# The first pixels of a spatial-reduction attention kernel, loaded by two queues in place of one

## The chip, the core and the metric

The kernel runs on one core of a Trainium2 chip. The core has a matrix engine (TensorE, PE in the profile), a vector engine (VectorE, DVE), an engine for activation functions (ScalarE, ACT), a general engine (GpSimd, POOL) and SyncE (SP), which mostly issues DMAs. DMAs are issued by an engine into its own queue (SP's, ACT's and POOL's appear below) and are moved by 16 DMA engines. The metric is the device time of one execution in microseconds (us): the median of several runs.

## What is computed

The reference has two stages. The first is attention with spatially reduced keys: `kv` (4 images of 384 x 32 pixels, 128 channels) is averaged over blocks of 4 x 4 pixels, which leaves 768 keys per image, and multiplied by `w_sr`; the result is keys and values at once.

```python
kv_pool = kv.reshape(B, H // r, r, W // r, r, C).mean(axis=(2, 4))
kv_flat = kv_pool.reshape(B, -1, C) @ w_sr
k = v = kv_flat
s = scale * (q @ k.transpose(0, 2, 1))
a = softmax(s)                      # with 1e-09 added to the sum
out = a @ v
```

The second stage is a feed-forward layer over all 4 x 12288 = 49152 rows: `h = x @ w_in` (128 to 2048), `g = h * sigmoid(1.702 h)`, `g @ w_out` (2048 to 128). Inputs and output are float32; the kernel computes in bf16 with float32 sums.

## The kernel before

The rows are worked in 96 groups of 512. A group's attention has six chunks of 128 keys: one matmul per chunk gives scores (L398), ACT takes their exponential (L400), and matmuls with the values, which carry a column of ones for the sum, follow (L412). The feed-forward stage has 16 chunks of 128 hidden units per group (L674, ACT's activation at L676, L684). Two rounds alternate: attention for half of the groups, then their feed-forward stage, then the same for the other half. ACT's work is a row of large activations, each of two or three banks of PSUM; PE fills the banks of one while ACT reads those of another. The order of all instructions is written out by the program itself: a planner with estimated costs places small jobs (pooling, transposing q, keys and values) between the large ones, and each engine executes its instructions strictly in the order in which they were written.

The change lies at the very beginning. The keys of image 0 are made from six chunks of pixels, each 128 rows of 2048 values (4 rows of 4 pixels make a key). Chunk 0 is loaded as float32 by SP's queue (L287) into `first_f`, a part of the big tile `x`, and cast to bf16 by DVE and ACT in five pieces (`cast_first`, L320 to L326): DVE casts columns 0 to 512, 512 to 1024 and 1792 to 2048, ACT casts 1024 to 1536 and 1536 to 1792. Behind it SP's queue loads `w_sr` (L289). All else is loaded by POOL's queue, which casts on the way: the first pieces of q (`load_q`, L264) and chunks 1 to 5 (`load_chunk`, L143), in this order: q group 0, q group 1, chunk 1, q groups 2 and 3, q groups 4 and 5, chunks 2 to 5.

While the loads are under way DVE makes an identity matrix and a matrix `sum4` that adds four rows (L304 to L318), and PE runs 13 matmuls on ones (`warm`, L335). Then the order on PE is:

- pool chunk 0 (16 matmuls at L152, four for each quarter of the columns, in the order of quarters 0, 2, 1, 3), transpose q group 0 (L278), one warm matmul, the keys of chunk 0 (L184), transpose q group 1;
- scores of group 0 with chunk 0 (L398), the values of chunk 0 (L189), one warm matmul, scores of group 1 with chunk 0 (L398);
- pool chunk 1 (L152), two warm matmuls, keys and values of chunk 1 (L197, L198), one warm matmul, transpose q group 2, scores of groups 0 and 1 with chunk 1 (L398), and so on.

On DVE the result of each of these is copied out of PSUM: `pTc` (L155), `kT` (L185, L199), `v` (L190, L200), `qT` (L284; for group 0 the copy is ACT's, L282). ACT's order at the beginning: load of its function table, the two casts of L325, the copy of L282, the exponentials of groups 0 and 1 with chunk 0 (512 columns each), then exponentials of 1024 columns.

Completion of a DMA is told by a semaphore; DMAs of SP's and ACT's queues take eight such semaphores in turn.

Of the kernel before, what the change touches and what calls it, by code (L numbers as in the profile page):

```python
# [24 lines left out]
def kernel(  # L25
    ctx, tc, q, kv, w_sr, moe_w_in, moe_w_out, out,
):
    nc = tc.nc
# [26 lines left out]
    kv_r = kv.rearrange("b (ch p) (a w) c -> b a ch p (w c)", p=128, a=2)  # L55
# [228 lines left out]
            nc.vector.tensor_copy(dst, src)  # L284

    first_f = x[:, 0:2 * SG].bitcast(F32)
    nc.sync.dma_start(out=first_f, in_=kv_r[0, 0, 0])  # L287
    w_sr_f = kvs[:, 0, 0, :]
    nc.sync.dma_start(out=w_sr_f, in_=w_sr)  # L289
    load_q(0, 0, 1)  # L290
# [23 lines left out]
    for m in range(0, 128, 32):  # L314
        p = slice(m, m + 32)
# [655 lines left out]
```

## Time and profile before

| what | value |
|---|---|
| time, median of 3 runs | 945.8 us (945.44 to 945.89) |
| span of the profiled execution | 943.6 us (the page gives no other time of it) |
| PE busy | 936.7 us, 99% of the span |
| ACT busy | 929.0 us, 98% |
| DVE busy | 688.6 us, 73% |
| POOL busy | 66.9 us, 7% |
| DMA, mean over the span | 106 GB/s |
| load of chunk 0, SP's queue | 1024 KB, 4.8 us from issue to landing |
| load of chunk 1, POOL's queue | landed 7.0 us after its issue at 2.52 us |
| ACT's first exponential | 8.38 us |
| ACT's third exponential | 12.00 us, after 2.32 us without work |

The profile is of one execution; times in it count from the start of the span. A row of the timeline has the start, the duration, the engine and the line, the operation with its output and input, how many instructions the row merges, and in brackets how long the engine had idled before and what ended that. A row of the chain has a start, a duration, and what the end of the kernel was waiting for in that time. Ends of matmuls are modelled: back to back ones overlap in their tails.

### The profile page before, as it was taken

Reading aid. Unit: us, or ns where it says so; the run is one execution under the profiler, and the core shown is the slowest. Engines: PE = TensorE matmul, PEld = TensorE weight load, DVE = VectorE, ACT = ScalarE, POOL = GpSimd, SP = SyncE. Lnnn points to the kernel's source line nnn. Section 1 sums busy time; section 2 is a strip of 40 time slices with the busy share of each in tenths; the row PEclk is TensorE's granted clock in tenths of the full one; section 3 lists DMA queues with packets and bytes.
Section 4 is the critical chain, followed back from the end, with each engine's and each line's share of the span. In section 5 each row is a group of like instructions: output and inputs, shape, how many; then the busy total and the mean of one; then the engine's idle time right before and its main releaser. Section 6 shows DMA issues by size and latency. Waiting matters only on the chain.

```text
span 943.6 us, 15502 instructions
## 1 busy us (share of the span) xinstructions
PE 936.7 (99%) x6218; PEld 499.8 (53%) x6218; DVE 688.6 (73%) x1261; ACT 929.0 (98%) x722; POOL 66.9 (7%) x117
## 2 busy tenths in 40 slices
PE   8999999999999999999999999999999999999998
PEld 4777776444444444445447777744444444444444
DVE  5677755767667788878787657588988779877851
ACT  6999999999999999999999999999999999999997
POOL 3101014200003320000000000000000000000000
PEclk9999999999999999999999999999999999999999
DMA  9998999947679993665235674462222121222222
GB/s 211 240 277 161 180 174 117 133 88 168 132 138 177 171 121 65 106 108 102 56 57 113 129 163 97 106 123 43 37 37 42 34 45 34 41 39 38 41 37 53
DMA packets 379464, 99.91 MB, mean 106 GB/s; under 512 B 353536, under 2 KB 376960, under 8 KB 378272
## 3 DMA queue, kind: packets, MB, share of 16 engines
q1 hardware_dynamic: 350784, 64.06, 36.2%
q0 software_dynamic: 28336, 34.74, 21.9%
q8 instruction: 48, 0.79, 0.3%
q14 instruction: 24, 0.20, 0.1%
q10 hardware_dynamic: 272, 0.13, 0.0%
HBM read 52.49 MB, written 49.81 MB: 108 GB/s over the span
## 4 chain that ended last, share of the span: by engine, by line
PE 92%; ACT 6%; DVE 1%; DMA 1%; issue 0%; POOL 0%; POOLq 0%
PE banks L684 35%; PE banks L674 35%; PE banks L412 11%; PE banks L398 9%; ACT ag L400 6%; DMA x<-in_kv_dram 1%; PE banks L469 1%; PE banks L463 1%; PE banks L712 0%; PE banks L152 0%; DVE x L443 0%; DVE ea L503 0%; PE banks L197 0%; POOL x L264 0%; PE banks L278 0%
## 5 line engine op out<-in xcount | busy, mean ns | idle before, releaser
L676 ACT ACTIVATE ag<-banks 128x1536 bf16<-128x1536 f32 (+1 forms) x506 | 676.3, 1510 | 0.0
L674 PE MATMUL banks<-x,w_both 128*128 128x512 bf16 x1509 | 408.2, 379 | 0.2 <-ACT ag L400 0.2
L684 PE MATMUL banks<-ag,w_both 128*128 128x512 bf16 x1493 | 405.5, 379 | 0.0
L400 ACT ACTIVATE ag<-banks 128x1536 bf16<-128x1536 f32 (+2 forms) x208 | 245.7, 1409 | 3.7 <-PE banks L398 3.2
L684 PEld LDWEIGHTS <-w_both 128*128 128x128 bf16 x1520 | 148.6, 98 | 179.0
L674 PEld LDWEIGHTS <-w_both 128*128 128x128 bf16 x1509 | 146.6, 98 | 172.0 <-issue 0.7
L412 PEld LDWEIGHTS <-ag 128*128 128x128 bf16 x2264 | 146.8, 98 | 47.9 <-issue 0.2
L412 PE MATMUL banks<-v,ag 128*128 128x129 bf16 x2264 | 166.0, 220 | 0.0
L398 PE MATMUL banks<-qT,kT 128*128 128x512 bf16 x542 | 150.8, 379 | 1.1 <-DVE kT L199 0.4
L695 DVE STREAM_TRANSPOSE o_sb<-banks 128x512 f32<-128x512 f32 x95 | 66.9, 705 | 70.4 <-PE banks L684 68.5
L503 DVE SCALAR_TENSOR_TENSOR ea<-ea,eb 128x512 f32<-128x512 f32 x136 | 93.0, 684 | 5.4 <-issue 2.1
L534 DVE RECIPROCAL eb<-ea 128x256 f32<-128x256 f32 x54 | 92.5, 1729 | 0.9
L527 DVE SCALAR_TENSOR_TENSOR ea<-ea,eb 128x512 f32<-128x512 f32 x108 | 73.8, 684 | 2.9
L440 DVE RECIPROCAL rec<-banks 128x3 f32<-128x3 f32 x122 | 21.8, 178 | 68.4 <-PE banks L412 67.8
L443 DVE TENSOR_TENSOR x<-banks,rec 128x384 bf16<-128x384 f32 x122 | 67.9, 557 | 4.2
L398 PEld LDWEIGHTS <-kT 128*128 128x128 bf16 x542 | 45.7, 97 | 20.8 <-issue 1.2
L514 DVE TENSOR_SCALAR qT<-banks 128x512 f32<-128x512 f32 x27 | 18.7, 692 | 39.5 <-PE banks L463 39.5
L492 DVE TENSOR_SCALAR ea<-banks 128x512 f32<-128x512 f32 x34 | 23.5, 691 | 29.1 <-PE banks L469 29.0
L209 POOL DMA_DIRECT2D kvs<-in_kv_dram x32 | 40.3, 1260 | 56.9 <-DMA kvs<-in_kv_dram 56.4
L697 POOL DMA_DIRECT2D out_dram<-o_sb x2 | 1.3, 674 | 519.1 <-DVE o_sb L695 519.1
L584 POOL MEMSET gate_tile<- 1x1 f32 x38 | 8.1, 214 | 285.4 <-DVE gate_tile L583 285.3
L498 DVE SCALAR_TENSOR_TENSOR eb<-eb,ea 128x512 f32<-128x512 f32 x34 | 23.5, 690 | 1.0
(95 smaller groups left out, 355.2 us busy)
## 6 DMA issues: line engine op xcount, KB each, us to landing
out_dram<-o_sb SPq DMA_DIRECT2D x378, 64.0 KB, 1.9
kvs<-in_kv_dram POOLq DMA_DIRECT2D x32, 384.0 KB, 6.6
q_bf<-in_q_dram POOLq DMA_DIRECT2D x21, 512.0 KB, 9.3
x_bf<-x SPq DMA_DIRECT2D x13, 768.0 KB, 5.5
x<-in_kv_dram POOLq DMA_DIRECT2D x6, 512.0 KB, 12.5
x<-in_kv_dram POOLq DMA_DIRECT2D x3, 1024.0 KB, 11.0
x_bf<-x SPq DMA_DIRECT2D x6, 384.0 KB, 4.0
x<-in_kv_dram SPq DMA_DIRECT2D x1, 1024.0 KB, 4.8
```

What stands on the lines that cost most here:

```text
L209: nc.gpsimd.dma_start(out=kv_sums[b][:, i2], in_=kv_p[b, i, w, :, i2], **({"accum_op": ADD} if n else {}))
L398: nc.tensor.matmul(ps[:, k, :], kTs[i // GB][:, jc * 128:(jc + 1) * 128], rhs, start=True, stop=True)
L400: nc.scalar.activation(place([("a",) + c for c in chunks]), ps, AF.Exp, scale=scale)
L412: nc.tensor.matmul(av_of[u][:, k * (C + 1):(k + 1) * (C + 1)], weights(("a", i, jc))[:, o:o + T], vs[i // GB][:, jc, 0:C + 1], start=(jc = ...
L443: nc.vector.tensor_tensor(to, ps[:, :, 0:C], rec.unsqueeze(2).broadcast_to([128, TS, C]), MUL)
L503: nc.vector.scalar_tensor_tensor(a, a, COEFFS[k], b, ADD, MUL)
L527: nc.vector.scalar_tensor_tensor(a, a, COEFFS[k], b, ADD, MUL)
L534: nc.vector.reciprocal(b[:, m:m + 256], a[:, m:m + 256])
L674: nc.tensor.matmul(ps[:, k, :], w_in_sb[:, fc * 128:(fc + 1) * 128], x[:, g % (4 * XS) * G:(g % (4 * XS) + 1) * G], start=True, stop=True)
L676: nc.scalar.activation(place([("m",) + c for c in chunks]), ps, AF.Gelu_apprx_sigmoid)
L684: nc.tensor.matmul(o_of[g], w_out_sb[:, fc, :], weights(("m", g, fc)), start=(fc == 0), stop=(fc == FCH - 1))
L695: nc.vector.transpose(o_sb, o_of.pop(g))
```

## The change

The 128 rows of the load of chunk 0 are issued as two DMAs of 64 rows: rows 0 to 63 by SP's queue as before, rows 64 to 127 by ACT's queue, which stands ahead of all other work of ACT. Nothing else is edited.

```diff
     first_f = x[:, 0:2 * SG].bitcast(F32)
-    nc.sync.dma_start(out=first_f, in_=kv_r[0, 0, 0])
+    for queue, p in ((nc.sync, slice(0, 64)), (nc.scalar, slice(64, 128))):
+        queue.dma_start(out=first_f[p], in_=kv_r[0, 0, 0][p])
     w_sr_f = kvs[:, 0, 0, :]
     nc.sync.dma_start(out=w_sr_f, in_=w_sr)
     load_q(0, 0, 1)
```

In the changed program every line behind the edit has a number that is higher by one.

## The prediction

> **What bounds the kernel now.** I read the engine table first, then the timeline of the first 16 us, the waits, and the chain that ended last.
>
> ```profile
> PE 936.7 (99%) x6218; PEld 499.8 (53%) x6218; DVE 688.6 (73%) x1261; ACT 929.0 (98%) x722; POOL 66.9 (7%) x117
> ```
>
> ScalarE (ACT) and TensorE (PE) are both full; ACT's idle time is 943.6 - 929.0 = 14.6 us. The timeline shows where most of that lies, around these lines:
>
> ```profile
> 0.75 1.28 ACT L325 ACT_TABLE_LOAD   x1 [0.75 <-PEq L955]
> 0.75 0.41 SPq L287 DMA_DIRECT2D x<-in_kv_dram  x1
> ...
> 5.61 0.93 ACT L325 CAST x<-x 128x512 bf16<-128x512 f32 x2 [3.58 <-DMA x<-in_kv_dram]
> 5.61 0.98 DVE L325 CAST x<-x 128x512 bf16<-128x512 f32 x3 [2.18 <-DMA x<-in_kv_dram]
> ...
> 6.90 0.29 DVE L155 CAST pTc<-banks 128x128 bf16<-128x128 f32 x1 [0.17 <-PE banks L152]
> ...
> 8.38 1.29 ACT L400 ACTIVATE ag<-banks 128x512 bf16<-128x512 f32 x2 [0.67 <-PE banks L398]
> ...
> 8.65 0.39 PE L398 MATMUL banks<-qT,kT 128*128 128x512 bf16 x1
> ...
> 9.56 0.56 PE L152 MATMUL banks<-sum,x 128*128 128x32 bf16 x16 [0.52 <-DMA x<-in_kv_dram]
> ...
> 12.00 4.73 ACT L400 ACTIVATE ag<-banks 128x1024 bf16<-128x1024 f32 x5 [2.32 <-PE banks L398]
> ```
>
> The bracket is the idle time before the row and what ended it. ACT idles 0.75 + 3.58 + 0.59 (before the L282 copy) + 0.67 + 2.32 = 7.9 us before 12.00, and about 5.95 us behind 937.4 (2.70 before its last copy, and from the end of that copy at 940.35 to the end of the span). From 12.00 to 937.4 only 14.6 - 7.9 - 5.95 = 0.7 us are left. So whatever moves the exponential at 12.00 moves the end of the kernel, nearly one to one; what moves anything earlier counts only as far as it moves that one. What sets 12.00, by the chain:
>
> ```profile
> 2.52 7.00 DMA x<-in_kv_dram
> 9.52 0.05 issue
> 9.56 0.56 PE banks L152 x16
> 10.13 0.54 PE banks L335 x2
> 10.66 0.16 PE banks L197
> ```
>
> This is the load of chunk 1 by POOL's queue, not the load that is changed (chunk 0). The two meet on PE: its instructions stand in order, so L152 for chunk 1 comes behind everything that chunk 0 needs, the last of which is the score matmul at 8.65. Two such matmuls in a row take 0.60 for 0.39 each, so one holds the array 0.21 us and PE could have begun L152 at 8.86. It began at 9.56. **Chunk 0 therefore has 0.70 us to spare.**
>
> **The change part by part.** The load itself: the same 1 MB, the same rows, on two queues. Packets of SP's queue, counted up to 3.5, 4.25 and 5.0 us, are 50, 93 and 130; two of the last are of w_sr. So the 128 rows of 8 KB are through at about 5.0, and the landing is recorded at 0.75 + 4.8 = 5.55, some 0.55 later. From 4.25 to 5.0 some 35 rows of 8 KB pass, near 390 GB/s. POOL's queue has its first packet at 5.2, though it was issued at 1.29: it begins when the rows are through. The pixels thus already use the DMA engines nearly alone.
>
> The issue on ACT: the one DMA that ACT issues in this trace took 0.417 us (L723). It now stands ahead of the table load, in time in which ACT waits anyway: cost 0. SP's issue of w_sr cannot come later than now, and w_sr_sb (6.51) isn't on the path: 0. Later DMAs of SP turn to the next of eight completion semaphores; one transpose gets another wait, for a DMA of tens of us before: 0.
>
> **The added wait** is what matters. The first casts on DVE and on ACT now need both halves, and in the built program each has one wait of its own, the other standing ahead of it as a separate instruction. On DVE nothing lies between. On ACT the order becomes: issue of ACT's half; wait for SP's half; table load; cast, which waits for ACT's half. Before, the table load ran from 0.75 to 2.03, inside the wait for pixels. Now it begins when SP's half lands. Its price is 1.28 us, by this row and by the two later ones (1283 ns each at L676). Behind it in ACT's queue are the two casts of L325 (0.93 together), the copy of qT at L282 and all exponentials; PE's L152 waits for the third and fourth quarter of the pixels from those casts.
>
> Let X be the landing of SP's half. ACT's cast begins at X + 0.06 (5.61 - 5.55) + 1.28, and S, its delay, is X + 1.34 - 5.61 = X - 4.27. The rest of chunk 0 hangs on it link by link (last cast 6.54, pTc 6.90, kT 7.61, score matmul 8.65), so L152 for chunk 1 begins at the later of 9.56 and 8.86 + S.
> - Lower end of X: SP's 64 rows all go first. The 64th packet falls at 3.5 + 0.75 x 14/43 = 3.74, so X = 4.3, S = 0: no cost.
> - Upper end: the rows alternate to the end, X = 5.55, S = 1.28, L152 at 10.14, 0.58 late.
> - I take X = 5.4: SP issued at 0.75 and ACT, whose table load began at 0.75, is free at the same moment, so alternation is nearest; SP's queue may lead a little. S = 1.13, L152 at 9.99, **+0.43 us**.
>
> ACT's own half binds only if it lands after 5.4 + 1.34 = 6.74, 1.2 us later than the whole load now. DVE's casts would end at 6.6 to 6.8, before ACT's at 7.67. The two early exponentials, 8.38 to 9.67, slide to about 9.5 to 10.8, still before 12.4.
>
> Sum: 943.6 + 0.4 = 944.0 of span. The page has no time beside its span; the median of the three runs shown, 945.8, is 2.2 above it, and I keep that: **946.2 us**, 0.05% slower. For this kernel 0.2% (1.9 us) is about what can be told from no change, so my forecast is: no difference.
>
> [...]
>
> **Rivals.**
> 1. *Hidden altogether.* SP's half lands by 4.97 (S up to 0.70), so the chunk 1 load still sets L152. For it: SP's rows may be read first. Against: equal starts. Time 945.8 (945.6 to 945.9).
> 2. *Faster.* The load begins slowly: 20 packets by 2.75, where the later rate of 43 in 0.75 us would have given 57 from 1.75 on. If that ramp is one queue's and two fill it, the rows end up to 37/57 = 0.65 us sooner, POOL's queue begins sooner and chunk 1 lands at 8.87. With X = 4.75, S = 0.48, PE is ready at 9.34: L152 0.22 earlier, 945.6; with SP's half well ahead too, 0.65, 945.15. Against: the ramp may be the memory's, and POOL's queue may find two queues ahead of it.
> 3. *The table load costs more than its row.* Working it as a cost of twice its row, S = 1.13 + 1.28 = 2.41, L152 at 11.27, +1.7, 947.5. Against: at 141.50 a table load follows an activation that ended at 141.48, and the next begins at 142.79; nothing but 1.28 us shows. [...]
> 4. *Slower by more than 0.2%, by PE's clock.* The 13 first matmuls (L335) start 0.43 apart until 3.90 and then about 0.21 apart: PE starts at half speed and takes 2.9 us of work to leave it. They end at 5.35; now PE does four small matmuls and waits some 1.1 us for ACT's first cast, where before its gap was 0.73. If that sends it back to half speed, 2.9 us of work at half speed loses 1.45, and about twice that if it comes in the dense stretch behind 12 and needs a second such stretch: 946.2 + 1.45 to 2.9 = 947.7 to 949.1. It decides from the gap at which the clock falls; gaps of 0.7 us at 5.35 and 8.9 left it up in this trace. [...]
>
> **How the numbers follow.** Forecast (+0.1 to +0.9) 0.62; hidden 0.16; faster rival 0.08; dearer table load 0.05; clock 0.09. The clock case and a little of the third lie above 947.7: slower by over 0.2%, 0.10. Even the faster rival stays within 0.2%; 0.02 for faster. The rest, 0.88, is within. The range goes from the middle of the faster rival, 945.3, past the forecast's upper end (946.4, and 0.3 for the scatter of 945.44 to 945.89) to half of the third, 947.1; it leaves out about 0.04 below and 0.13 above.
>
> **What would show it.** The table load on ACT at 5.3 to 5.6 instead of 0.75, and the cast behind it near 6.7. L152 of chunk 0 with a wait of about 1 us for ACT in its middle. L152 for chunk 1 near 10.0, waiting for PE's own order and not for a DMA; the exponential at 12.4. ACT full from there on. The prediction is wrong if the table load still stands before the wait, if SP's half lands below 5.0, if chunk 1 lands more than 0.4 us away from 9.52, or if the matmuls between 6 and 12 stand 0.43 apart.

## The result: slower by 0.37%, and the profile after

The changed kernel takes 948.46 us (five executions: 948.05, 948.19, 948.46, 950.75, 950.98) against 945.89 before (the median of five); the ratio is 1.0037, with a 95% interval of 1.0026 to 1.0047. The executions fall into two groups, near 948.2 with a mean granted PE clock of 0.998 and near 950.8 with 0.996. The profiled one took 950.75 and has a span of 949.0, 5.4 us above that of before. Its beginning, from the timeline (lines of the changed program are higher by one):

```profile
0.76 0.56 ACTq L288 DMA_DIRECT2D x<-in_kv_dram  x1
0.76 0.58 SPq L288 DMA_DIRECT2D x<-in_kv_dram  x1
...
8.67 1.28 ACT L326 ACT_TABLE_LOAD   x1 [8.67 <-DMA x<-in_kv_dram]
8.70 1.02 DVE L326 CAST x<-x 128x512 bf16<-128x512 f32 x3 [5.27 <-DMA x<-in_kv_dram]
...
9.97 0.93 ACT L326 CAST x<-x 128x512 bf16<-128x512 f32 x2
10.64 0.49 PEld L152 LDWEIGHTS <-x 128*128 128x128 bf16 x12 [1.29 <-ACT x L326]
...
13.99 0.61 PE L399 MATMUL banks<-qT,kT 128*128 128x512 bf16 x1
...
14.39 0.63 PE L152 MATMUL banks<-sum,x 128*128 128x32 bf16 x16
...
17.52 1.02 ACT L401 ACTIVATE ag<-banks 128x1024 bf16<-128x1024 f32 x1 [2.28 <-PE banks L278]
```

The table load has moved behind the wait, as forecast. But the wait ends at 8.6, where it ended at 5.55. ACT's third exponential stands at 17.52 in place of 12.00: 5.52 late, and the span is 5.4 longer. That this exponential carries the end nearly one to one was right.

The issues with their times to landing show which half is late:

```profile
x<-in_kv_dram ACTq DMA_DIRECT2D x1, 512.0 KB, 5.2
x<-in_kv_dram SPq DMA_DIRECT2D x1, 512.0 KB, 7.8
```

SP's 512 KB needed 7.8 us where the whole 1024 KB needed 4.8. Packets by queue (count, MB, share of the time of 16 DMA engines) say why; a packet is counted in the stretch in which it starts. Before, from 3.25 to 4.25 us:

```profile
q1 hardware_dynamic: 54, 0.44, 106.4%
```

After, from 3.25 to 4.25 us (q10 is ACT's queue):

```profile
q10 hardware_dynamic: 29, 0.23, 103.9%
```

After, from 5 to 6 us (q1 is SP's queue):

```profile
q1 hardware_dynamic: 27, 0.22, 101.2%
```

The time of one packet is the share times 16 engines times the stretch, over the count: 1.064 x 16 / 54 = 0.315 us before, 1.012 x 16 / 27 = 0.600 us after. The engines are as busy as before, and each 8 KB row takes nearly twice as long. Nor do the two queues run side by side: ACT's 64 rows have all started by 4.26 us, when SP's first starts, and SP's last starts near 6.7.

PE's clock, lastly (the columns are the stretch, busy times by engine, the granted clock, the DMA share and GB/s):

```profile
8.00:9.00 1.00, 0.00 (x0) 0.00 (x0) 0.30 (x1) 0.33 (x1) 0.00 (x0) 1.00 1.30 228
9.00:10.00 1.00, 0.27 (x4) 0.17 (x4) 0.85 (x4) 0.99 (x2) 0.90 (x2) 0.81 1.09 221
10.00:12.00 2.00, 1.36 (x17) 0.84 (x17) 0.32 (x2) 1.20 (x3) 0.39 (x2) 0.50 1.08 196
12.00:14.00 2.00, 2.00 (x10) 0.69 (x9) 1.27 (x4) 0.83 (x2) 1.19 (x2) 0.50 1.26 216
14.00:16.00 2.00, 2.00 (x21) 0.85 (x21) 0.29 (x1) 0.65 (x2) 0.51 (x1) 0.50 1.07 215
16.00:18.00 2.00, 1.82 (x13) 0.92 (x15) 1.40 (x4) 0.48 (x1) 0.57 (x2) 0.89 1.06 213
```

From about 9.6 to 16.5 PE runs at half speed; before, the column has 1.00 in all of the first 18 us. The column does not show the slow start, in which it has 1.00 as well. The warm matmuls do (before, then after):

```profile
0.96 4.39 PE L335 MATMUL banks<-ones 128*32 128x512 bf16 x13 [0.96 <-DVE col L307]
0.97 5.55 PE L336 MATMUL banks<-ones 128*32 128x512 bf16 x13 [0.97 <-DVE col L308]
```

Before, they begin 0.43 apart and from 3.90 about 0.21 apart; here all thirteen lie 0.43 apart, so PE had not left half speed when the last of them began.

### The profile page after: what moved, and what is told of

The parts are those of the page before. It is cut to its first block, busy times and chain, and to the rows that moved or that the text cites. A ratio compares the mean times of both kernels' runs of the same rounds, so it can differ in the third digit from the quotient of the medians.

```text
span 949.0 us, 15391 instructions
## 1 busy us (share of the span) xinstructions
PE 933.4 (98%) x6104; PEld 500.8 (53%) x6218; DVE 689.1 (73%) x1261; ACT 929.1 (98%) x722; POOL 66.8 (7%) x117
## 4 chain that ended last, share of the span: by engine, by line
PE 55%; ACT 42%; DVE 1%; DMA 1%; issue 1%; ACTq 0%
ACT ag L677 36%; PE banks L685 18%; PE banks L675 17%; PE banks L413 9%; PE banks L399 9%; ACT ag L401 6%; DMA x<-in_kv_dram 1%; PE banks L464 0%; PE banks L713 0%; PE banks L278 0%; PE banks L336 0%; DVE x L444 0%; PE banks L152 0%; PE banks L470 0%; DVE ea L504 0%
## 5 line engine op out<-in xcount | busy, mean ns | idle before, releaser
L675 PE MATMUL banks<-x,w_both 128*128 128x512 bf16 x1468 | 403.0, 379 | 1.7 <-ACT ag L401 0.2
L685 PE MATMUL banks<-ag,w_both 128*128 128x512 bf16 x1465 | 399.9, 379 | 1.8
L399 PE MATMUL banks<-qT,kT 128*128 128x512 bf16 x497 | 145.7, 379 | 2.5 <-DVE kT L199 0.4
```

Of the source, the lines that this page charges most:

```text
L399: nc.tensor.matmul(ps[:, k, :], kTs[i // GB][:, jc * 128:(jc + 1) * 128], rhs, start=True, stop=True)
L675: nc.tensor.matmul(ps[:, k, :], w_in_sb[:, fc * 128:(fc + 1) * 128], x[:, g % (4 * XS) * G:(g % (4 * XS) + 1) * G], start=True, stop=True)
L685: nc.tensor.matmul(o_of[g], w_out_sb[:, fc, :], weights(("m", g, fc)), start=(fc == 0), stop=(fc == FCH - 1))
```

## The experiments

Open were: whether two queues or two halves of 64 rows make the rows slow, and what of 64 rows; what the table load behind the wait costs; and what PE's clock costs. Diffs are against the changed kernel unless said otherwise.

**Halves on one queue, columns on two, alternate rows on two.** These three and the next ran on one chip, where the kernel before took 945.48.

Both halves on SP's queue:

```diff
-    for queue, p in ((nc.sync, slice(0, 64)), (nc.scalar, slice(64, 128))):
+    for queue, p in ((nc.sync, slice(0, 64)), (nc.sync, slice(64, 128))):
```

> Both halves of 64 rows are issued by SP's queue, one behind the other. Theory R (a DMA into 64 adjacent partitions moves each 8 KB row in about 0.6 us per DMA engine in place of 0.31 to 0.38, whichever queue it is on): the 128 rows are through at 6.2 to 6.8 us, the second half lands at 6.8 to 8.6, and the time is 947 to 951 us. Theory Q (two hardware queues at once are what is slow): the rows are through at 5.0 to 5.3, the second half lands at 5.5 to 5.8, and only the table load behind the wait is left, 945.8 to 946.5 us.

950.59 us, ratio 1.0054 (1.0040 to 1.0068). One queue is no faster than two. Its packets from 3.25 to 4.25 us:

```profile
q1 hardware_dynamic: 28, 0.21, 95.1%
```

0.951 x 16 / 28 = 0.54 us. The table load begins at 9.58, later than the forecast of this run.

All 128 rows on both queues, cut by columns:

```diff
-    for queue, p in ((nc.sync, slice(0, 64)), (nc.scalar, slice(64, 128))):
-        queue.dma_start(out=first_f[p], in_=kv_r[0, 0, 0][p])
+    for queue, c in ((nc.sync, slice(0, SG // 2)), (nc.scalar, slice(SG // 2, SG))):
+        queue.dma_start(out=first_f[:, c], in_=kv_r[0, 0, 0][:, c])
```

> The same two queues, but each loads 1024 of the 2048 columns of all 128 rows (pieces of 4 KB). ACT's casts need ACT's half alone, so the table load stands before the wait again. Theory R: both halves land by 5.8 us and the time is 945.3 to 946.2. Theory Q: the second half lands at 7 us or later and the time is 947 to 950.

945.56 us, ratio 1.0001 (0.9993 to 1.0010): no different from before. Its packets (4 KB) from 3.25 to 4.25 us and its issues:

```profile
q1 hardware_dynamic: 53, 0.22, 54.2%
q10 hardware_dynamic: 50, 0.20, 50.7%
```

```profile
x<-in_kv_dram ACTq DMA_DIRECT2D x1, 512.0 KB, 5.0
x<-in_kv_dram SPq DMA_DIRECT2D x1, 512.0 KB, 5.2
```

0.542 x 16 / 53 = 0.164 us for 4 KB, the speed of before, with both queues at work. Two queues do no harm here; loads of 64 neighbouring rows do.

Even rows on SP, odd rows on ACT:

```diff
-    for queue, p in ((nc.sync, slice(0, 64)), (nc.scalar, slice(64, 128))):
+    for queue, p in ((nc.sync, slice(0, 128, 2)), (nc.scalar, slice(1, 128, 2))):
```

> Two queues with 64 rows each, but even rows on SP and odd rows on ACT, so each DMA reaches over all partitions. Theory R, where it is the adjacency: rows of 8 KB in 0.31 to 0.38 us, both halves landed by 5.8, and with the table load behind the wait 945.9 to 946.6 us. Theory Q, or a cost of 64 rows as such: landing at 7 us or later, 947.5 to 951 us.

952.53 us, ratio 1.0074 (1.0061 to 1.0086). By its time this was a miss, but the time is another thing's: with strided rows POOL's loads were made to wait for the pixels, and POOL's first issue moved from 1.30 to 7.01. The rows themselves are fast, 0.853 x 16 x 0.5 / 23 = 0.30 us on ACT's queue from 3.5 to 4.0 us:

```profile
q10 hardware_dynamic: 23, 0.18, 85.3%
```

So 64 rows as such are not slow, though SP's half landed at 6.4, later than expected, since ACT's half again went first. But POOL was silent here, which the later runs had to take apart.

**The table load early.**

```diff
+    early_table = cpool.tile([128, 1], F32)
+    nc.vector.memset(early_table, 0.0)
+    nc.scalar.copy(early_table, early_table)
```

> The changed kernel with a copy of one column by ACT ahead of the casts, so the table load runs at about 1.4 us and only the casts wait. If the table load behind the wait is paid in full: 1.28 us faster than the changed kernel of the same clock, 946.7 to 947.3 (949.4 to 949.8 where PE's clock has fallen). If it is hidden: 948.0 to 951.0 as the changed kernel.

948.66 us, ratio 1.0032 (1.0019 to 1.0044). The table load runs at 1.37 and the casts begin at 8.17, right at the landing. The two executions with a clock of 0.996 took 948.8, 2.0 less than the changed kernel's of that clock, of which 0.5 is an earlier landing in the profiled one (8.1 against 8.6). The three at 0.998 took 947.92 to 948.66, where the changed kernel took 948.05 to 948.46: no gain. So the table load's 1.28 is seen in one group at most. That group lies 0.6 to 1.0 below what was expected for a table load paid in full, the other 0.6 and more above it.

**What the clock and the landing cost.** These and the next two ran together; before took 945.50.

```diff
-    warm(13)
+    warm(26)
```

> The changed kernel with 26 in place of 13 warm matmuls, so PE has work until 8 or 9 us. If PE's half clock costs what the profile of the changed kernel shows (some 1.9 us of the 5.5 by which its third exponential is late): the clock stays up, the third exponential stands near 15.6, and all executions lie at 948.0 to 949.1 us, with none at 950.8. If the clock costs nothing: two groups again, 948.2 and 950.8.

949.36 us, ratio 1.0038 (1.0026 to 1.0051), four executions at 949.27 to 949.57 and one, with a clock of 1.0, at 948.17. A miss in part: the extra matmuls reach 8.47, but PE then waits 1.2 us for ACT's cast, and the clock still falls, at 11.3 in the profile, where the third exponential stands at 16.26. None stands at 950.8.

With the table load early as well, and 22 warm matmuls:

```diff
+    early_table = cpool.tile([128, 1], F32)
+    nc.vector.memset(early_table, 0.0)
+    nc.scalar.copy(early_table, early_table)
...
-    warm(13)
+    warm(22)
```

> The changed kernel with the table load early and 22 warm matmuls: only the slow landing of the halves is left. From a landing at 8.1 to 8.5 us: chunk 0 is 2.5 to 2.9 late, 0.7 of it spare, so 947.0 to 947.7 us; the kernel with the warm matmuls alone should lie 1.0 to 1.3 above it. If the landing is not what costs: at or below 946.

948.28 us, ratio 1.0029 (1.0018 to 1.0041); five of six executions have a clock of 1.0. What is left is the landing, at 8.56 in the profile:

```profile
8.63 0.93 ACT L329 CAST x<-x 128x512 bf16<-128x512 f32 x2 [5.79 <-DMA x<-in_kv_dram]
...
14.35 6.78 ACT L404 ACTIVATE ag<-banks 128x1024 bf16<-128x1024 f32 x7 [1.64 <-PE banks L278]
...
21.66 1.02 ACT L404 ACTIVATE ag<-banks 128x1024 bf16<-128x1024 f32 x1 [0.54 <-PE banks L152]
```

The time is 0.6 above the range expected. The casts are 3.02 late, so chunk 0 should let PE go at 8.86 + 3.02 = 11.88; L152 for chunk 1 stands at 11.91, and the exponential is 2.35 late. (Chunk 1's own load, issued at 2.52, landed 9.3 later, at 11.82, so here both ends meet.) A second cost had not been seen: ACT idles 0.54 at 21.66, because the pooling at 20.62 (chunk 3) waits 0.90 for its load. POOL's queue starts behind the slow rows, so its later chunks are late too. 2.35 + 0.54 = 2.89, and the span is 946.6 against 943.6. The kernel with the warm matmuls alone lies 1.1 above this one by its median, as expected, but four of its five executions had a spell of half clock; the one at a clock of 1.0 took 948.17, no more than this kernel's 948.03 to 948.39. At equal clock the table load's cost is not seen here.

**The table load alone.** Columns again, but cut at 1280, so that ACT's first cast (columns 1024 to 1536) needs both loads:

```diff
-    for queue, c in ((nc.sync, slice(0, SG // 2)), (nc.scalar, slice(SG // 2, SG))):
+    for queue, c in ((nc.sync, slice(0, 1280)), (nc.scalar, slice(1280, SG))):
```

(against the kernel with columns)

> Columns again (1280 on SP, 768 on ACT, all 128 rows), but cut so that ACT's first cast needs both loads: the table load stands behind the wait while the pixels land as fast as before. By the prediction's own sum (SP's part landing at 5.5 to 5.8, S of 1.2 to 1.5, 0.7 spare): 0.4 to 0.9 us slower than before, 945.9 to 946.4. If the table load's place costs nothing: 945.3 to 945.8. If it costs by itself what the changed kernel lost: 947.5 or more.

946.82 us, ratio 1.0010 (1.0001 to 1.0019), in two groups. The four executions with a clock of 1.0 took 945.61 to 945.86, 0.1 to 0.4 above before. The seven at 0.998 took 946.77 to 947.09, 1.3 to 1.6 above. The profiled one (947.09) shows both costs:

```profile
5.83 1.28 ACT L326 ACT_TABLE_LOAD   x1 [5.83 <-DMA x<-in_kv_dram]
7.12 0.93 ACT L326 CAST x<-x 128x512 bf16<-128x512 f32 x2
...
14.10 16.23 ACT L401 ACTIVATE ag<-banks 128x1024 bf16<-128x1024 f32 x17 [2.20 <-PE banks L278]
```

```profile
9.00:10.00 1.00, 0.83 (x7) 0.26 (x5) 0.88 (x3) 0.22 (x1) 0.00 (x0) 0.74 1.19 199
10.00:11.00 1.00, 1.00 (x4) 0.23 (x3) 0.33 (x3) 0.60 (x1) 0.71 (x1) 0.50 1.24 204
11.00:12.00 1.00, 1.00 (x18) 0.65 (x17) 0.27 (x1) 0.60 (x1) 0.52 (x1) 0.50 1.27 227
12.00:13.00 1.00, 1.00 (x5) 0.22 (x3) 0.02 (x1) 0.00 (x0) 0.42 (x1) 0.55 1.03 209
```

By 0.74 and 0.55 the half speed lasts from 9.48 to 12.90, 3.4 us. This is the case that the prediction had described, pixels landing nearly as fast as before and a table load behind the wait. With the clock up it costs 0.1 to 0.4, under the 0.4 to 0.9 expected, and three of those four executions lie in the range expected for no cost at all; with a spell of half clock it costs more than 0.9. In the profiled execution the casts are 7.12 - 5.61 = 1.51 late, which the prediction's sum turns into 0.81 at the third exponential. That one is 2.10 late, so the spell is worth 1.29 there; the span is 1.7 longer, so 0.4 is made up behind it.

**What of 64 rows is slow.** Four loads of 32 rows on SP's queue:

```diff
-    for queue, p in ((nc.sync, slice(0, 64)), (nc.scalar, slice(64, 128))):
+    for queue, p in [(nc.sync, slice(n, n + 32)) for n in (0, 32, 64, 96)]:
```

> Four loads of 32 rows on SP's queue. Theory R (the speed goes by how many neighbouring partitions one load reaches): 8 KB rows at about 1.2 us per DMA engine, all rows through at 11 to 12 us, time 952 to 958 us. If the number of DMAs costs, and not their reach: 8 KB rows in 0.3 to 0.6 us, all through by 7.5, time 947 to 951.

951.30 us, ratio 1.0060 (1.0046 to 1.0074). Not 1.2 us: from 5 to 6 us 0.18 MB, or 22 rows of 8 KB, took 75.6% of 16 engines, 0.55 us each. The speed does not simply go by how many neighbours one load reaches.

Three kernels, run once each, took destination, source and POOL apart. The first sends even source rows to partitions 0 to 63 and odd ones to 64 to 127:

```diff
-    for queue, p in ((nc.sync, slice(0, 64)), (nc.scalar, slice(64, 128))):
-        queue.dma_start(out=first_f[p], in_=kv_r[0, 0, 0][p])
+    for queue, p, row in ((nc.sync, slice(0, 64), slice(0, 128, 2)), (nc.scalar, slice(64, 128), slice(1, 128, 2))):
+        queue.dma_start(out=first_f[p], in_=kv_r[0, 0, 0][row])
```

> Even rows of the pixels go to partitions 0 to 63 (SP), odd rows to partitions 64 to 127 (ACT): adjacent in the chip's memory as in the changed kernel, alternate in the source. The keys of chunk 0 are then sums over other rows than the reference's; the work and its shapes are the same. Three theories of the slow rows. R-chip (64 adjacent partitions as the destination): 8 KB rows in about 0.6 us. R-source (64 adjacent rows as the source): 0.31 us, pixels landed by 5.8. R-pool (POOL's loads, issued meanwhile, disturb loads of 64 rows; in the alternate-rows run POOL waited for the pixels before its first load): about 0.6 us. Time 947 to 951 us where the rows are slow, 945.6 to 947 where not.

The second sends rows 0 to 63 to the even partitions and 64 to 127 to the odd ones:

```diff
-    for queue, p, row in ((nc.sync, slice(0, 64), slice(0, 128, 2)), (nc.scalar, slice(64, 128), slice(1, 128, 2))):
+    for queue, row, p in ((nc.sync, slice(0, 64), slice(0, 128, 2)), (nc.scalar, slice(64, 128), slice(1, 128, 2))):
```

(against the one before it)

> The reverse: rows 0 to 63 of the source to the even partitions (SP), rows 64 to 127 to the odd ones (ACT); again other sums than the reference's. POOL waits for the pixels here before its first load, as in the alternate-rows run. R-chip: 0.31 us for a row of 8 KB. R-source: 0.6 us. R-pool: 0.31 us. The time, 951 to 954 us, tells little, because of POOL's wait.

The third holds POOL back in the changed kernel:

```diff
+    held = cpool.tile([128, 1], F32)
+    nc.gpsimd.tensor_copy(held, first_f[:, 0:1])
```

> The changed kernel (adjacent rows to adjacent partitions, two queues) with a copy of one column by POOL ahead of its loads, so POOL issues nothing until the pixels have landed. R-chip and R-source: 0.6 us for a row of 8 KB. R-pool: 0.31 us. Time 953 to 957 us where the rows are slow.

They took 948.69, 951.98 and 953.65 us; the kernel before took 945.47 on that chip. Adjacent partitions, from 5 to 6 us (ACT's half; SP's went first here):

```profile
q10 hardware_dynamic: 27, 0.22, 101.9%
```

Adjacent source rows, from 4 to 4.75 us:

```profile
q1 hardware_dynamic: 37, 0.30, 95.6%
```

POOL held, from 5 to 6 us:

```profile
q1 hardware_dynamic: 28, 0.23, 104.0%
```

That is 0.604, 0.310 and 0.594 us for a row. The source's order does not matter and POOL does not; which partitions a load writes does.

The halves exchanged between the queues:

```diff
-    for queue, p in ((nc.sync, slice(0, 64)), (nc.scalar, slice(64, 128))):
+    for queue, p in ((nc.scalar, slice(0, 64)), (nc.sync, slice(64, 128))):
```

> The changed kernel with the halves exchanged between the queues: rows 0 to 63 on ACT's, 64 to 127 on SP's. If the queue decides which half is moved first: ACT's half is through at about 4.3 us again and SP's near 6.6, 948.0 to 951.0 us. If the rows decide: SP's half goes first, the table load can begin near 5.3, and the time is 1 to 2 us better, 946.5 to 949.5.

948.94 us, ratio 1.0038 (1.0024 to 1.0052), on the same chip; ACT's half went first again, and SP's landed 7.9 us after its issue. In the run with adjacent partitions SP's went first, though, so neither the queue nor the rows settle it.

Last, 64 adjacent partitions that reach across partition 64. If 64 neighbours as such are slow, SP's rows take 0.6 us here; if what counts is that all of them lie on one side of partition 64, 0.31. The time is then 947 to 951 us or 946 to 949.5, with the table load behind the wait:

```diff
-    for queue, p in ((nc.sync, slice(0, 64)), (nc.scalar, slice(64, 128))):
+    for queue, p in ((nc.sync, slice(32, 96)), (nc.scalar, slice(0, 32)), (nc.scalar, slice(96, 128))):
```

> Rows 32 to 95 on SP's queue in one load, rows 0 to 31 and 96 to 127 on ACT's in two. The destination of SP's load is 64 adjacent partitions, as in the changed kernel, but it crosses partition 64. [...]

949.04 us, ratio 1.0040 (1.0025 to 1.0054). From 3.5 to 4.0 us SP's rows run alone:

```profile
q1 hardware_dynamic: 20, 0.16, 82.1%
```

0.821 x 16 x 0.5 / 20 = 0.33 us: full speed. From 4.25 to 4.75 us SP's rows are again the only ones to start:

```profile
q1 hardware_dynamic: 16, 0.13, 116.0%
```

But these took 1.16 x 16 x 0.5 / 16 = 0.58 us each, and so did its first 16 nearly (from 2.25 to 3.25 us, 54.8%, 0.55 us each). In the order of their starts, SP's first 16 rows took 0.55, the next 32 0.36 in the mean (from 3.25 to 4.25 us, 71.9%) and the last 16 0.58; the mean of all is 0.46. So 64 neighbours are slow (0.60) when all lie on one side of partition 64; when they lie on both, some run at full speed (0.33) and some do not (0.58). The time, inside both of these ranges, does not decide. ACT's two loads, each on one side, ran in turn with SP's rows; that they slowed the others is likely but not shown. Side by side, a row took 0.60 us in the halves, 0.55 in the quarters and 0.30 at every other partition; why one side of partition 64 is slow was not shown.

## Why the prediction was wrong

- **The step that failed is X**, the landing of SP's half. The prediction took 5.4 us, between 4.3 and 5.55, and it was 8.56. Both ends were made of the same assumption: that the rows are the same work however they are cut, so that the halves together cannot take longer than the whole. At 0.60 us for a row in place of 0.315 they do. The last row started at 6.7 instead of 4.9, and the landing came 1.9 behind that start instead of 0.6 (the prediction's "through at about 5.0" is a count of starts). The packet counts of before could not show this: each load of pixels there writes all 128 partitions.
- **A second input was wrong**, for the same reason: chunk 1's landing, which the sum holds at 9.52. POOL's queue begins when the last rows have started, with its first packet between 6.6 and 6.7 in place of 5.2. Its load of chunk 1, issued at 2.52 as before, has this line after:

```profile
x<-in_kv_dram POOLq DMA_DIRECT2D x1, 512.0 KB, 9.1
```

  It lands at 11.6, 2.1 later than before, beyond the 0.4 that the prediction named as a sign of being wrong. In the profiled execution the casts are later still, so it does not set the end there. But whatever is done for the table load or the casts, L152 for chunk 1 cannot begin before some 11.65 when the rows are this slow. That is an estimate of a floor of 2.1 us under the loss. It fits that no run with halves or quarters took less than 947.9; no run tried it by itself.
- **The formula held as far as it was tested.** S = X - 4.27 is 4.29 us for X = 8.56; the cast stood at 9.97, 4.36 late. With the table early and PE warm, a delay of 3.02 gives 11.88 for L152 and the trace has 11.91. But chunk 1's own landing gives 11.87 there, so that run does not test the 0.70 us to spare. That the third exponential carries the end one to one held here (5.52 and 5.4); in five other profiled runs, the one with the table load alone among them, the span grew by some 0.4 less.
- **The table load** moved as forecast and took 1.28 us. Alone, with pixels about as fast as before, it cost 0.1 to 0.4 us while the clock stayed up; the sum had 0.43. In the run with adjacent partitions SP's half went first, the case of the lower end of X: the table load began at 5.95 and was over by 7.23, but ACT's own half, slow as well, held the cast until 8.35. The dearer table load (third rival) is not seen, and no run shows the cost of twice its row that the range was partly made from: the cast begins 1.30 after the load's start, at 9.97.
- **The clock** (fourth rival, 0.09) came true, and not by the gap of 1.1 us alone: PE has no matmul from 6.52 to 9.19. In the profiled execution it is worth 17.52 - (12.00 + 4.29 - 0.70) = 1.93 us of the 5.52, inside the rival's 1.45 to 2.9. Its "2.9 us of work" to leave half speed is no fixed amount: here twelve warm matmuls, 5.1 us of work, were not enough. Its chance was too low: by their mean clocks it fell in all five executions of the changed kernel, and with the table load alone, where PE's longest wait was 1.15 us, in 7 of 11.
- **Where the loss went**, then, in the profiled execution: landing 3.01, table load 1.28, less 0.70 to spare, clock 1.93: 5.52 at the exponential, 5.4 in the span. These are terms along one chain; taking some of them away gives back at most what lies above the floor of chunk 1's load. The executions near 948.2 had a spell of half clock too, by their mean of 0.998: in all four kernels whose profiled execution has this mean the spell lasts some 3.4 us (by the clock's column 11.3 to 14.7 with 26 warm matmuls and 9.48 to 12.90 with the table load alone; in the other two matmuls of 512 columns take 0.61 us in place of 0.39 from 10.7 to about 14.1) and, by the sum above, is worth 1.1 to 1.3 us; at 0.996 (the changed kernel, both halves on one queue, the table load early, the quarters) it lasts 6.8 by the column. With the profiled landing they would lose some 4.8 us, and their spans grew by 2.7 to 3.1. Their landing is not known, so this difference stays open. If SP's half went first in them, as in the run with adjacent partitions (0.998, 948.69 us), part of the table load would be hidden and they would lie near that; this was not shown.
- **The faster rival** rested on a slow start that two queues would fill. With two queues at full speed (columns) the pixels landed at 5.75 and 5.95, no sooner than before: the slow start is not one queue's.

The verdict "no difference" was wrong: 2.6 us is more than the 1.9 us that it allowed. No version beat the kernel before; the cut by columns equals it.

## What to carry to other kernels

A load that is cut into two by rows is not two halves of the same work: look at which partitions each part writes (0.60 against 0.31 us for a row here), and compare the time of one packet (share x engines x stretch / count), not only the bytes. If a load must be split, a cut by columns kept all 128 partitions in each part and cost nothing here (945.56 against 945.48 us). Ask also which loads queue up behind the slow one: here the next chunk was 2.1 us late. A wait that is added to an engine's first instruction can also push what used to run ahead of it, here a table load, from 0.75 to 8.67, behind the wait; and a gap on PE near the start of a dense stretch may cost more through its clock than through its length: with the table load alone, an estimated 1.29 us through the clock against 0.81 through the late casts.

## What the runs showed of the hardware that was not expected

- 64 partitions on one side of partition 64: 0.60 us for an 8 KB row; all 128 or every other one: 0.30 to 0.32; 32 to 95, beside loads of one side: 0.46, of which some at 0.33.
- Two loads of 64 rows, issued at the same moment by SP and ACT, were hardly interleaved: all or most of one queue's rows had started before the other's first (in the changed kernel, 4.26 and 4.25 us). ACT's went first in the changed kernel, SP's in one run with the same instructions and another source.
- The semaphore of a slow half came 1.9 us behind the start of its last row, where the load before has 0.6. The load of rows 32 to 95 has 2.0, so one side alone does not explain it. Why was not tried.
- PE's spells of half clock lasted some 3.4 us in the four profiled executions with a mean clock of 0.998 and 6.8 in four of the five with 0.996; with alternate rows (0.995) it went from 10.5, by the column, to about 20.7, by the lengths of the matmuls. The changed kernel's two groups of times, 0.998 and 0.996, go with the first two of these means.
- PE's clock fell near 9.5 us with the table load alone (0.74 from 9 to 10, 0.50 from 10 to 11), where PE's longest wait was 1.15 us.
